# Seven block products for eight in a gated feed-forward layer, with its summed weights streamed from DRAM and GpSimd taken out of the work

## The chip, the cores and the metric

One core of one Trainium2 chip runs the kernel. The metric is device time in microseconds of one execution; the median of three runs stands for a kernel. A profiled execution of its own gives the trace.

## The reference, cut to what matters

Three stages follow each other on 2 x 3008 = 6016 tokens of 256 features, in float32.

```python
X = rfft(x, axis=1)                       # x: (2, 3008, 256)
Yr = Xr @ w_r - Xi @ w_i + b_r            # complex linear map in frequency space
Yi = Xr @ w_i + Xi @ w_r + b_i
y  = irfft(shrink(Yr, 0.01) + 1j * shrink(Yi, 0.01))
x  = y.reshape(6016, 256)
h  = x @ moe_w_in                         # first part, 2048 hidden
x  = (h * clip(h + 3, 0, 6) / 6) @ moe_w_out
g  = x @ moe2_w_gate                      # second part, 1536 hidden
out = (g / (1 + exp(-g)) * (x @ moe2_w_val)) @ moe2_w_out
```

`shrink(a, l)` is `sign(a) * max(abs(a) - l, 0)`.

## The kernel before, in words

The kernel has a Fourier stage (forward transform, complex linear map, inverse transform, up to about 172 us) and then two feed-forward parts. Tokens of the feed-forward parts come in 12 blocks: eleven of 512 and one of 384. Every product of the two parts is made of three float32r matmuls, from operands that are split in a high and a low half: low weight by high data, high weight by low data, high by high (`mm3`, lines 103 to 106). A weight tile is 128 x 128 and the moving operand is one block of up to 512 tokens.

The first part has 16 slices f of 128 hidden features. A unit (block, f) runs `project1` (line 386: two `mm3` into a PSUM tile `ph`, a Relu on ScalarE, a multiply on VectorE), then `lower` (line 434: the high half by a ScalarE copy, the low half by a subtraction), then `outp` (line 445: two `mm3` into the two accumulators `acc`). The second part has 12 slices, and `project2` (line 407) makes four `mm3` (gate and value, each over the two halves of the 256 input features), so with `outp` a unit takes 18 matmuls. In the loop at line 487 a unit's `outp` is issued after the `project` of the unit two later. `rounds` (line 459) lets the parts alternate: first part of block 0, first part of block 1, second part of block 0, first part of block 2, and so on. `post` (line 371) makes the input of a block of the first part from the Fourier stage's result, with 12 to 14 small float32 matmuls for each half of the features.

All weights come as 64-bit words and are converted on the chip (`Convert`, line 125): a load, a Square on ScalarE (the mask), four VectorE instructions of 256 columns (`words`, lines 152 to 156), a high half by a ScalarE copy, and a low half by a GpSimd subtraction (line 164). The 32 pieces of the first part's weights (`conv1`) are converted during the Fourier stage, one step in each `ln` (line 272) and in each late `pre`. The 36 pieces of the second part's weights (`conv2`) are converted one in each unit from the start of the first part, and while this lasts `lower` puts its subtraction on GpSimd (line 441). In the Fourier stage GpSimd also makes `yp`, the subtraction at the end of `ln` (line 293). All weights then stay in SBUF.

The order in which each engine works is the program order (the schedule is written out by hand). The Fourier stage goes through twelve steps p (`ORDER`, line 307): `ln(p, 0)`, `ia(p-1, 0)`, two halves of `s2(p+1)`, `ln(p, 1)`, `ia(p-1, 1)`. In `s2` (line 248) ScalarE makes the high half `xh` and its negative, VectorE the low half `xl`, and ScalarE the negative of `xl`; this last one is put ahead of the next function by `run` (line 265), so that the second half's `xh` stands behind it in ScalarE's queue.

Of the kernel before, what the change touches and what calls it, by code (L numbers as in the profile page):

```python
# [9 lines left out]
F32 = mybir.dt.float32  # L10
# [21 lines left out]
BLK = 512  # L32

# [41 lines left out]
def fourier_moe_kernel(ctx: ExitStack, tc: tile.TileContext, x, lin, bias, w1, w2, fwd1, inv2, fwd2,  # L75
# [6 lines left out]
    ps = ctx.enter_context(tc.tile_pool(name="ps", bufs=1, space=PSUM))  # L82
    dram = ctx.enter_context(tc.tile_pool(name="scratch", bufs=1, space=DRAM))
    Bd = [dram.tile([GW, NJ * DIM], F32, name=f"Bd{b}") for b in range(NB)]
    Cd = [dram.tile([GW, NJ * DIM], F32, name=f"Cd{b}") for b in range(NB)]

# [35 lines left out]
    w1p = pool(ctx, "w1", "right")  # L122
    W1, W2 = {}, {}

    class Convert:
# [21 lines left out]
        def words(self, i):  # L147
# [8 lines left out]
            v.scalar_tensor_tensor(out=tf, in0=m, scalar=LEAST * LEAST, in1=tf, op0=ALU.is_ge, op1=ALU.mult)  # L156
            self.full[i] = tf
# [114 lines left out]
    def ln(b, Q, h):  # L272
# [20 lines left out]
        nc.gpsimd.tensor_tensor(out=yp[b, Q, h], in0=yb, in1=yc, op=ALU.subtract)  # L293
# [51 lines left out]

    blocks = [(t, min(t + BLK, TOK)) for t in range(0, TOK, BLK)]

# [9 lines left out]
    ct, xs1, xs2, acc, state = {}, {}, {}, {}, {}  # L357
# [40 lines left out]
    def finish1(k, n):  # L398
        a = acc.pop((1, k))
        xs2[k] = pair(xb_p, "xb")  # L400
        for e in range(2):
            hi, lo = (t[:, e, :n] for t in xs2[k])
            nc.scalar.mul(hi, a[e][:, :n], 1.0 / 6.0)
            nc.vector.scalar_tensor_tensor(out=lo, in0=a[e][:, :n], scalar=1.0 / 6.0, in1=hi.bitcast(F32),  # L404
                                           op0=ALU.mult, op1=ALU.subtract)

    def project2(k, f, n):
        xh, xl = xs2[k]
        wh, wl = W2[f]
        pg = bank([128, BLK], "pg")  # L410
        pv = bank([128, BLK], "pv")
        for j, p in ((0, pg), (1, pv)):
            for dh in range(2):
                w = (slice(None), j, slice(dh * 128, dh * 128 + 128))
                mm3(p[:, :n], wh[w], wl[w], xh[:, dh, :n], xl[:, dh, :n], dh == 0, dh == 1)
        r = xs_p.tile([128, 512], F32, tag="r", name="r", bufs=3)
        nc.scalar.activation(r[:, :n], pg[:, :n], AF.Silu)  # L417
        nc.vector.tensor_tensor(out=r[:, :n], in0=r[:, :n], in1=pv[:, :n], op=ALU.mult)  # L418
        return r

    def finish2(k, n):
        a = acc.pop((2, k))
        t0 = k[0]
        for e in range(2):
            o = xs_p.tile([128, 512], F32, tag="r", name="osb", bufs=3)
            if e == 0:
                nc.scalar.copy(o[:, :n], a[e][:, :n])
            else:
                nc.vector.tensor_copy(o[:, :n], a[e][:, :n])
            nc.sync.dma_start(out[e * 128 : e * 128 + 128, t0 : t0 + n], o[:, :n])  # L430

    PART = {1: (KF1, project1, finish1, W1, 1), 2: (KF2, project2, finish2, W2, 2)}

    def lower(u):
        n = ntok(u[1])
# [4 lines left out]
        busy = conv1.done() and not conv2.done()  # L440
        (nc.gpsimd if busy else nc.vector).tensor_tensor(  # L441
            out=lo[:, :n], in0=g[:, :n], in1=hi[:, :n].bitcast(F32), op=ALU.subtract)
        state[u] = (hi, lo)

    def outp(u):
        part, k, f = u
        nf, _, finish, W, col = PART[part]
        n = ntok(k)
        if f == 0:
            acc[part, k] = [acc_bank([128, BLK], f"acc{e}") for e in range(2)]  # L450
# [4 lines left out]
        if f == nf - 1:  # L455
            finish(k, n)

    NBK = len(blocks)
    rounds = [(1, 0)]
    for n in range(NBK):  # L460
        if n + 1 < NBK:
# [84 lines left out]
```

## Time and profile before

| | |
|---|---|
| median of 3 runs | 1309.83 us (1308.58 to 1311.1) |
| the profiled execution | 1310.21 us, of which 1308.4 us are its span from first to last instruction |
| mean granted TensorE clock | 0.993 |
| busy: TensorE, VectorE, ScalarE, GpSimd | 98%, 51%, 42%, 11% of the span |

The profile's durations of matmuls overlap, because matmuls are pipelined, so a stretch in which TensorE is shown busy throughout can still hold more or fewer matmuls. The pace is read from the starts of successive matmuls.

### The profile page before, as it was taken

To read this page: it belongs to the slowest core of one execution; us is meant where nothing else is said; L and a number is where in the kernel's file an instruction comes from. 1 tells how busy PE (TensorE), PEld (TensorE's weight loads), DVE (VectorE), ACT (ScalarE), POOL (GpSimd) and SP (SyncE) were. 2 spreads that over 40 slices of the span, in tenths; PEclk is the share of its full clock that TensorE was granted. 3 is DMA by queue.
4 is the path that set the end of the run, shared out by engine and by line. 5 is a ranking of instruction groups with operands and counts; after the bars stand their busy time and mean duration, and the time that the engine had idled before them with its cause. 6 is when DMAs were issued, how large, how long until landed. Compare 5 with 4: busy or idle time off the path is not lost.

```text
span 1308.4 us, 15775 instructions
## 1 busy us (share of the span) xinstructions
PE 1280.3 (98%) x6124; PEld 1070.1 (82%) x6124; DVE 673.0 (51%) x1054; ACT 550.4 (42%) x982; POOL 149.9 (11%) x146
## 2 busy tenths in 40 slices
PE   7889999999999999999999999999999999999998
PEld 2689977678888888888888888888888888889888
DVE  2687889994543543534534434434434435435433
ACT  2345556563433433433433434434434424424332
POOL 1144457763000000000000000000000000000000
PEclk9899999999999999999999999999999999999999
DMA  8866532230100100001001001001001001000000
GB/s 281 272 210 201 171 116 79 79 91 1 35 1 1 38 1 16 20 1 38 1 1 35 1 1 38 1 1 35 1 1 35 1 1 32 1 1 17 1 17 13
DMA packets 33099, 61.42 MB, mean 47 GB/s; under 512 B 2928, under 2 KB 15568, under 8 KB 33024
## 3 DMA queue, kind: packets, MB, share of 16 engines
q1 hardware_dynamic: 26464, 53.43, 13.2%
q10 hardware_dynamic: 6336, 6.29, 1.4%
q8 instruction: 48, 0.79, 0.3%
q0 software_dynamic: 224, 0.69, 0.2%
q14 instruction: 27, 0.22, 0.1%
HBM read 41.66 MB, written 18.74 MB: 46 GB/s over the span
## 4 chain that ended last, share of the span: by engine, by line
PE 85%; DVE 9%; issue 3%; DMA 1%; ACT 1%; POOL 0%; SPq 0%; DVEq 0%; ACTq 0%; POOLq 0%
PE acc L105 10%; PE acc L106 10%; PE acc L104 10%; PE ph L106 5%; PE ph L104 5%; PE ph L105 5%; PE pg L104 5%; PE pg L106 5%; PE pv L104 5%; PE pg L105 5%; PE pv L106 5%; PE pv L105 5%; PE p L380 2%; DVE wt L153 2%; DVE wt L154 2%
## 5 line engine op out<-in xcount | busy, mean ns | idle before, releaser
L439 ACT CAST gh<-r 128x512 fp32r<-128x512 f32 (+1 forms) x336 | 205.5, 612 | 274.6 <-DVE r L418 156.6
L441 DVE TENSOR_TENSOR gl<-r,gh 128x512 fp32r<-128x512 f32 (+1 forms) x297 | 201.7, 679 | 174.5 <-ACT gh L439 173.6
L418 DVE TENSOR_TENSOR r<-r,pv 128x512 f32<-128x512 f32 (+1 forms) x144 | 97.4, 676 | 231.7 <-PE pv L106 231.7
L395 DVE SCALAR_TENSOR_TENSOR r<-r,ph 128x512 f32<-128x512 f32 (+1 forms) x192 | 129.7, 676 | 109.3 <-ACT r L394 109.3
L394 ACT ACTIVATE r<-ph,three 128x512 f32<-128x512 f32 (+1 forms) x192 | 130.3, 679 | 110.0 <-PE ph L106 101.8
L105 PE MATMUL acc<-gl,w1h 128*128 128x512 f32 (+1 forms) x384 | 149.9, 390 | 4.1 <-POOL gl L441 1.7
L104 PE MATMUL ph<-xah,w1l 128*128 128x512 f32 (+1 forms) x384 | 148.9, 388 | 0.0
L104 PE MATMUL acc<-gh,w1l 128*128 128x512 f32 (+1 forms) x384 | 147.8, 385 | 0.7 <-DVE xbl L404 0.7
L105 PE MATMUL ph<-xal,w1h 128*128 128x512 f32 (+1 forms) x384 | 148.2, 386 | 0.0
L106 PE MATMUL ph<-xah,w1h 128*128 128x512 f32 (+1 forms) x384 | 148.1, 386 | 0.0
L106 PE MATMUL acc<-gh,w1h 128*128 128x512 f32 (+1 forms) x384 | 147.9, 385 | 0.0
L417 ACT ACTIVATE r<-pg 128x512 f32<-128x512 f32 (+1 forms) x144 | 85.0, 590 | 147.1 <-PE pg L106 143.6
L104 PE MATMUL pg<-xbh,w2l 128*128 128x512 f32 (+1 forms) x288 | 112.6, 391 | 0.0
L106 PE MATMUL pg<-xbh,w2h 128*128 128x512 f32 (+1 forms) x288 | 110.9, 385 | 0.0
L104 PE MATMUL pv<-xbh,w2l 128*128 128x512 f32 (+1 forms) x288 | 110.8, 385 | 0.0
L105 PE MATMUL pg<-xbl,w2h 128*128 128x512 f32 (+1 forms) x288 | 110.8, 385 | 0.0
L106 PE MATMUL acc<-gh,w2h 128*128 128x512 f32 (+1 forms) x288 | 110.8, 385 | 0.0
L106 PE MATMUL pv<-xbh,w2h 128*128 128x512 f32 (+1 forms) x288 | 110.8, 385 | 0.0
L105 PE MATMUL acc<-gl,w2h 128*128 128x512 f32 (+1 forms) x288 | 110.8, 385 | 0.0
L105 PE MATMUL pv<-xbl,w2h 128*128 128x512 f32 (+1 forms) x288 | 110.7, 384 | 0.0
L104 PE MATMUL acc<-gh,w2l 128*128 128x512 f32 (+1 forms) x288 | 110.7, 384 | 0.0
L105 PEld LDWEIGHTS acc<-gl,w1h 128*128 128x128 f32 x384 | 72.0, 188 | 25.5 <-POOL gl L441 12.1
(66 smaller groups left out, 1903.4 us busy)
## 6 DMA issues: line engine op xcount, KB each, us to landing
st<-in_w SPq DMA_DIRECT2D x68, 256.0 KB, 2.7
x<-in_x SPq DMA_DIRECT2D x16, 384.0 KB, 5.5
Bd<-bs SPq DMA_DIRECT2D x16, 384.0 KB, 4.4
z<-Bd SPq DMA_DIRECT2D x12, 512.0 KB, 6.0
Cd<-cs ACTq DMA_DIRECT2D x12, 512.0 KB, 5.6
out_t<-osb SPq DMA_DIRECT2D x22, 256.0 KB, 2.0
ct<-Cd SPq DMA_DIRECT2D x6, 576.0 KB, 4.5
ct<-Cd SPq DMA_DIRECT2D x4, 672.0 KB, 4.8
```

Source lines behind the costliest of these rows:

```text
L104: nc.tensor.matmul(o, wl, xh, start=start, stop=False)
L105: nc.tensor.matmul(o, wh, xl, start=False, stop=False)
L106: nc.tensor.matmul(o, wh, xh, start=False, stop=stop)
L153: v.scalar_tensor_tensor(out=t, in0=L, scalar=29, in1=t, op0=ALU.logical_shift_right, op1=ALU.bitwise_or)
L154: v.scalar_tensor_tensor(out=t, in0=H, scalar=0xC0000000, in1=t, op0=ALU.bitwise_and, op1=ALU.bitwise_or)
L380: nc.tensor.matmul(p[:, a - k[0] : z - k[0]], ct[k][:, j - p0, eh * 128 : (eh + 1) * 128], inv2_sb[:, a - j * QN : z - j * QN], start=True ...
L394: nc.scalar.activation(r[:, :n], p[:, :n], AF.Relu, bias=three)
L395: nc.vector.scalar_tensor_tensor(out=r[:, :n], in0=r[:, :n], scalar=6.0, in1=p[:, :n], op0=ALU.min, op1=ALU.mult)
L417: nc.scalar.activation(r[:, :n], pg[:, :n], AF.Silu)
L418: nc.vector.tensor_tensor(out=r[:, :n], in0=r[:, :n], in1=pv[:, :n], op=ALU.mult)
L439: nc.scalar.copy(hi[:, :n], g[:, :n])
L441: (nc.gpsimd if busy else nc.vector).tensor_tensor(out=lo[:, :n], in0=g[:, :n], in1=hi[:, :n].bitcast(F32), op=ALU.subtract)
```

## The change

It does six things.

1. The first part runs over all blocks before the second part begins. Its result is stored as full float32 in a DRAM tensor `Xd` (two 256 KB stores for each block) and is loaded again, one pair of blocks at a time, for the second part. The last two blocks have 448 tokens each, in place of 512 and 384.
2. The second part takes pairs of blocks. For a slice f and a pair, gate and value by two halves of the input features form a 2 x 2 block matrix of weights, and two halves of the features by two blocks form a 2 x 2 block matrix of data. Their product is made of seven block products (Strassen, in Winograd's form) in place of eight, each an `mm3` as before, accumulated in three PSUM tags `P` (two banks), `Tb` and `Q`, with copies of intermediate sums in SBUF. `outp` is unchanged in kind: four `mm3` for a pair. So a `quad` (pair, f) takes 33 matmuls, where the two units took 36.
3. Sums of weights (four VectorE instructions of 128 columns for each slice) and their high and low halves are made once, during the first part, by one step in every second unit, and stored in DRAM tensors `Wd` (18 blocks of 128 x 128 for each slice, 1.18 MB). The second part loads a slice for each quad, 72 loads, into a ring of four buffers; the load for quad q+2 is issued at the start of quad q.
4. Sums of data (four VectorE subtractions, seven ScalarE copies and seven VectorE subtractions for each pair) are made during the pair before, at two places in each quad (`todo.send()`); those of the first pair are made in the last 28 units of the first part.
5. The subtractions on GpSimd go to VectorE: `Convert.low`, `yp`, and `lower` during the conversion.
6. PSUM and the first part's weights are released between the parts and taken again with new tags.

```diff
         def low(self, i):
-            nc.gpsimd.tensor_tensor(out=lo, in0=self.full.pop(i), in1=hi.bitcast(F32), op=ALU.subtract)
+            nc.vector.tensor_tensor(out=lo, in0=self.full.pop(i), in1=hi.bitcast(F32), op=ALU.subtract)
...
-        nc.gpsimd.tensor_tensor(out=yp[b, Q, h], in0=yb, in1=yc, op=ALU.subtract)
+        nc.vector.tensor_tensor(out=yp[b, Q, h], in0=yb, in1=yc, op=ALU.subtract)
...
+    pairs = [(t, min(t + 2 * BLK, TOK)) for t in range(0, TOK, 2 * BLK)]
+    blocks = [(a + (z - a) // 2 * i, a + (z - a) // 2 * (i + 1)) for a, z in pairs for i in range(2)]
...
-        busy = conv1.done() and not conv2.done()
-        (nc.gpsimd if busy else nc.vector).tensor_tensor(
-            out=lo[:, :n], in0=g[:, :n], in1=hi[:, :n].bitcast(F32), op=ALU.subtract)
+        low(lo[:, :n], g[:, :n], hi[:, :n])
...
+    units = [(k, f) for k in blocks for f in range(KF1)]
...
+            for f in range(KF2):                      # Convert2.steps, one step in every second unit
+                for what in range(3):
...
+                    self.words(i, self.full_of(i))
+                    yield
+                F = full.pop(f)
+                for o, x, y, op in ((4, 0, 3, ALU.add), (5, 4, 1, ALU.subtract), (6, 1, 0, ALU.subtract), (7, 2, 5, ALU.subtract)):
+                    nc.vector.tensor_tensor(out=F[:, o], in0=F[:, x], in1=F[:, y], op=op)
+                t = ring()
+                nc.scalar.copy(t[:, :7], F[:, 1:])
+                yield
+                O = full.pop((f, 2))
+                nc.scalar.copy(t[:, 14:16], O)
+                low(t[:, 7:14], F[:, 1:], t[:, :7])
+                yield
+                low(t[:, 16:], O, t[:, 14:16])
+                nc.sync.dma_start(Wd[f], t.bitcast(F32).rearrange("p a b -> p (a b)"))
+                yield
...
+    def fetch(q):
+        if q < len(quads):
+            slot[q] = ring()
+            nc.sync.dma_start(slot[q].bitcast(F32).rearrange("p a b -> p (a b)"), Wd[quads[q][1]])
...
+    w1_stack.close()
+    ps_stack.close()
...
+        def product(o, m, start=False):               # inside quad(q)
...
+            nc.tensor.matmul(o, wl, x[:, 0, :n], start=start, stop=False, skip_group_check=not start)
+            nc.tensor.matmul(o, wh, x[:, 1, :n], start=False, stop=False, skip_group_check=not start)
+            nc.tensor.matmul(o, wh, x[:, 0, :n], start=False, stop=True, skip_group_check=not start)
...
+        fetch(q + 2)
...
+        product(P, 1, start=True)
+        nc.scalar.copy(c1, P[:, :n])
+        product(T, 7, start=True)
+        nc.scalar.copy(c7, T[:, :n])
+        product(Q, 2, start=True)
+        nc.vector.tensor_tensor(out=v0, in0=Q[:, :n], in1=c1, op=ALU.add)
+        if before is not None:
+            (pb, fb), w, g = before
+            hi = split_hi(g[1], pb)
+            g[1] = (hi, split_lo(g[1], hi, pb))
+        product(P, 6)
+        nc.scalar.copy(cu, P[:, :n])
+        todo.send()
+        share(0, 0)
+        product(T, 4)
+        nc.vector.tensor_tensor(out=h, in0=T[:, :n], in1=cu, op=ALU.add)
+        nc.scalar.activation(s0[:, :n], h, AF.Silu)
+        share(0, 1)
+        product(P, 5)
+        nc.vector.tensor_tensor(out=h, in0=P[:, :n], in1=c7, op=ALU.add)
+        nc.scalar.activation(s1[:, :n], h, AF.Silu)
+        nc.vector.tensor_tensor(out=s0[:, :n], in0=s0[:, :n], in1=v0, op=ALU.mult)
+        hi = split_hi(s0, p)
+        g0 = (hi, split_lo(s0, hi, p))
+        todo.send()
+        share(1, 0)
+        share(1, 1)
+        product(P, 3)
+        nc.vector.tensor_tensor(out=s1[:, :n], in0=s1[:, :n], in1=P[:, :n], op=ALU.mult)
```

`share(t, e)` is one `mm3` of the quad before into accumulator (t, e); `split_hi` is a ScalarE copy and `split_lo` a VectorE subtraction.

## Rows read from the trace of the kernel before

**Rows 1.** The page: busy time and share of the span of each engine, number of instructions.

```profile
PE 1280.3 (98%) x6124; PEld 1070.1 (82%) x6124; DVE 673.0 (51%) x1054; ACT 550.4 (42%) x982; POOL 149.9 (11%) x146
```

**Rows 2.** Timeline of TensorE: start, duration, engine, line, operation; [idle before, releaser].

```profile
340.45 0.39 PE L104 MATMUL ph<-xah,w1l 128*128 128x512 f32 x1
...
343.17 0.39 PE L104 MATMUL ph<-xah,w1l 128*128 128x512 f32 x1
...
1284.14 0.33 PE L105 MATMUL pg<-xbl,w2h 128*128 128x384 f32 x1
...
1287.26 0.33 PE L105 MATMUL pg<-xbl,w2h 128*128 128x384 f32 x1
```

**Rows 3.** Timeline of TensorE, end of the Fourier stage to the second part's eighth slice.

```profile
171.44 1.40 PE L300 MATMUL p<-yp,n 128*128 128x256 f32 x4 [1.93 <-POOL yp L293]
172.28 0.99 PE L104 MATMUL ph<-xah,w1l 128*128 128x512 f32 x1
...
175.60 0.40 PE L105 MATMUL ph<-xal,w1h 128*128 128x512 f32 x1
...
304.62 1.65 PE L380 MATMUL p<-inv_sb,ct 96*128 96x10 f32 x14
```

**Rows 4.** Timeline, all engines, while the second part's weights are converted.

```profile
223.57 1.49 POOL L441 TENSOR_TENSOR gl<-r,gh 128x512 fp32r<-128x512 f32 x1 [0.79 <-POOL w2l L164]
223.94 1.40 DVE L156 SCALAR_TENSOR_TENSOR wt<-mask,wt 128x256 f32<-128x256 f32 x1
...
232.69 0.43 DVE L156 SCALAR_TENSOR_TENSOR wt<-mask,wt 128x256 f32<-128x256 f32 x1
...
236.02 0.50 PE L105 MATMUL acc<-gl,w1h 128*128 128x512 f32 x1 [0.98 <-POOL gl L441]
```

**Rows 5.** The chain that ended last, in the Fourier stage: start, duration, what.

```profile
95.93 0.87 PE p L300 x4
...
105.20 0.86 PE p L300 x4
...
150.90 0.61 DVE yb L289
...
160.37 0.61 DVE yb L289
```

**Rows 6.** Timeline of VectorE in one step of the Fourier stage.

```profile
126.76 0.68 DVE L289 TENSOR_TENSOR yb<-p,bias_sb 128x512 f32<-128x512 f32 x1
...
127.89 0.68 DVE L109 TENSOR_TENSOR xl<-p,xh 128x512 fp32r<-128x512 f32 x1
129.82 0.69 DVE L109 TENSOR_TENSOR xl<-p,xh 128x512 fp32r<-128x512 f32 x1 [1.25 <-ACT xh L259]
130.43 0.28 DVE L152 TENSOR_SCALAR wt<-st 128x256 uint32<-128x256 uint32 x1
...
132.01 0.68 DVE L289 TENSOR_TENSOR yb<-p,bias_sb 128x512 f32<-128x512 f32 x1
```

**Rows 7.** Groups by line and shape, whole span: count, busy us, mean ns, idle before.

```profile
L441 DVE TENSOR_TENSOR gl<-r,gh 128x512 fp32r<-128x512 f32 x269 | 186.1, 692 | 159.4 <-ACT gh L439 158.6
...
L418 DVE TENSOR_TENSOR r<-r,pv 128x512 f32<-128x512 f32 x132 | 90.8, 688 | 214.7 <-PE pv L106 214.7
...
L427 ACT COPY osb<-acc 128x512 f32<-128x512 f32 x11 | 6.5, 588 | 1.4 <-PE acc L106 1.2
```

**Rows 8.** Timeline of ScalarE: the Relu behind the matmuls of Rows 2.

```profile
342.07 0.69 ACT L394 ACTIVATE r<-ph,three 128x512 f32<-128x512 f32 x1 [0.66 <-PE ph L106]
```

**Rows 9.** DMA issues: count, KB each, median us from issue to landing.

```profile
ct<-Cd SPq DMA_DIRECT2D x4, 672.0 KB, 4.8
```

**Rows 10.** Stretches of 20 us: busy us (instructions) by engine, granted clock, DMA share, GB/s.

```profile
20.00:40.00 20.00, 12.70 (x39) 5.68 (x40) 5.95 (x11) 5.11 (x11) 0.00 (x0) 0.89 0.93 332
...
160.00:180.00 20.00, 18.07 (x102) 15.63 (x101) 17.40 (x29) 9.98 (x21) 9.38 (x10) 0.91 0.57 175
...
220.00:240.00 20.00, 17.71 (x72) 12.72 (x72) 19.42 (x32) 12.28 (x26) 13.86 (x12) 1.00 0.28 78
```

More of the change, by code (lines that the diff above doesn't have):

```diff
@@ L32 @@
 BLK = 512
+SLOT = 18
 EDGE = 480
@@ new lines, in fourier_moe_kernel, with operands, load, b @@
+    conv2 = Convert2([(w2[:, f, j], None, None) for f in range(KF2) for j in range(3)])
+    steps = conv2.steps()
+    B, raw = {}, {}
+    halves = [(z - a) // 2 for a, z in pairs]
+    xo = [cv, None]
+    def operands(p):
+        a, z = pairs[p]
+        n = halves[p]
+        def load():
+            raw[p] = cv.tile([128, 2, 2 * BLK], F32, tag="raw", name=f"raw{p}", bufs=1)
+            nc.sync.dma_start(raw[p][:, :, : z - a], Xd[:, :, a:z])
+        def b(k, t):
+            return raw[p][:, k, t * n : t * n + n]
+        B[p] = {}
+        T = {}
+        def sub(i, x, y):
+            T[i] = cv.tile([128, BLK], F32, tag="T", name=f"T{i}", bufs=3)
+            nc.vector.tensor_tensor(out=T[i][:, :n], in0=x(), in1=y(), op=ALU.subtract)
+        def hi(m, x):
+            B[p][m] = xo[p % 2].tile([128, 2, BLK], F32R, tag="xo", name=f"xo{m}", bufs=7)
+            nc.scalar.copy(B[p][m][:, 0, :n], x())
+        def lo(m, x):
+            low(B[p][m][:, 1, :n], x(), B[p][m][:, 0, :n])
+        def t(i):
+            return lambda: T[i][:, :n]
+        def r(k, j):
+            return lambda: b(k, j)
+        of = {1: r(0, 0), 5: t(1), 6: t(2), 4: t(4), 7: t(3), 2: r(1, 0), 3: r(1, 1)}
+        todo = [load, lambda: None]
+        subs = {5: (1, r(0, 1), r(0, 0)), 6: (2, r(1, 1), t(1)), 4: (4, r(1, 0), t(2)), 7: (3, r(1, 1), r(0, 1))}
+        for m, x in of.items():
+            if m in subs:
+                todo.append(lambda m=m: sub(*subs[m]))
+            todo.append(lambda m=m, x=x: hi(m, x))
+            todo.append(lambda m=m, x=x: lo(m, x))
+        return todo
@@ L487, in fourier_moe_kernel @@
+    def fetch(q):
+        if q < len(quads):
+            slot[q] = ring()
+            nc.sync.dma_start(slot[q].bitcast(F32).rearrange("p a b -> p (a b)"), Wd[quads[q][1]])
+    quads = [(p, f) for p in range(len(pairs)) for f in range(KF2)]
+    first = iter(operands(0))
     for n in range(len(units) + 2):
@@ L499, in fourier_moe_kernel, with sb @@
             conv1.step()
-        conv2.step()
+        elif n % 2 == 0:
+            next(steps, None)
+        left = len(units) + 2 - n
+        if left <= 28:
+            next(first, lambda: None)()
+        if left in (8, 4):
+            fetch(2 - left // 4)
+    assert next(steps, True) and next(first, None) is None
+    w1_stack.close()
+    ps_stack.close()
+    ps2 = ctx.enter_context(tc.tile_pool(name="ps2", bufs=1, space=PSUM))
+    p2 = pool(ctx, "p2", "right")
+    xo[1] = p2
+    def sb(tag, name, bufs):
+        return p2.tile([128, BLK], F32, tag=tag, name=name, bufs=bufs)
@@ L503, with __init__, send @@
+    class Todo:
+        def __init__(self):
+            self.steps = iter(())
+        def send(self):
+            next(self.steps, lambda: None)()
+    todo = Todo()
+    for q in range(len(quads) + 1):
+        if q < len(quads) and quads[q][1] == 0 and quads[q][0] + 1 < len(pairs):
+            todo.steps = iter(operands(quads[q][0] + 1))
+        quad(q)
 def kernel(x, w_r, w_i, b_r, b_i, moe_w_in, moe_w_out, moe2_w_gate, moe2_w_val, moe2_w_out):
```

171 lines of the change are left out of this document (109 added, 62 removed).

## The prediction

> **What bounds the kernel now.** I read the page first: TensorE is busy 98% of the span, no other engine over 51% [rows 1]. That share hides the pace, so the timeline of TensorE comes next, for starts of successive matmuls. In the undisturbed part 12 matmuls of 512 columns start in 343.17 - 340.45 = 2.72 us, 0.2267 us each, and 18 of 384 columns in 3.12 us, 0.1733 each [rows 2]. The difference is 0.417 ns a column, with 13 ns beside it for each matmul, so I reckon 0.200 us for 448 columns. At these paces the first part costs 192 x (11 x 0.2267 + 0.1733) = 512.0 us and the second 216 x (11 x 0.2267 + 0.1733) = 576.0 us. There TensorE alone sets the time.
>
> Two stretches are not of that kind. From the first `ph` matmul at 172.28 to the `post` at 304.62 there are two rounds of the first part and eight slices of the second, with their `outp` two units behind: 516 matmuls, 117.0 us, and two `post` halves of the length in [rows 3], 3.2 us after overlap. The stretch takes 132.3 us, so 12.1 are lost. Of these 1.7 are lost at the start: seven matmuls take 175.60 - 172.28 = 3.32 us instead of 1.59, right behind an idle time of 1.93 us [rows 3]. The other 10.4 are the conversion of the second part's weights: a VectorE instruction of 256 columns takes 0.43 us alone, but 1.40 us when it starts beside a GpSimd subtraction of 1.49 us, and ends just after it; TensorE then waits for the GpSimd low half [rows 4]. In such a stretch of 20 us 72 matmuls start, where the pace allows 88, though TensorE is shown busy 17.71 us [rows 10].
>
> The Fourier stage is the other. The chain of waits repeats there every 9.27 us through TensorE and later every 9.47 us through VectorE [rows 5]. So VectorE is about as near to the bound as TensorE.
>
> **The block products.** A quad takes 33 matmuls where two units took 36. Five pairs of 512-column halves and one of 448: 12 x 33 x (5 x 0.2267 + 0.200) = 528.0 us, against 576.0. Term: -48.0. The first part's matmuls cost 192 x (10 x 0.2267 + 2 x 0.200) = 512.0, as before, and the posts are the same work.
>
> This holds only if TensorE finds its operands in time, so I follow a quad in slots of one `mm3` (0.68 us): M1, M7, M2, M6, share, M4, share, M5, share, share, M3. A result can be read 0.26 us after the group's matmuls have issued (six from 340.45 end at 341.81, the Relu starts at 342.07) [rows 2, 8]. A ScalarE copy from PSUM takes 0.59, a VectorE addition from PSUM or a low half 0.69 [rows 7]. M6 adds into the bank that the copy `c1` reads: M1 ends at 0.68, the copy runs 0.94 to 1.53, M6 starts at 2.04; slack about 0.45. M5 needs `cu` (done 3.6) at 4.76. M3 needs the addition behind M5 (5.44): 5.70 to 6.39, and M3 starts at 6.80; slack about 0.35. The share of a quad's first half follows a quad later, with some 1.7 us to spare. In its queue VectorE has seven instructions of 0.69 and on average one more for `operands`, 5.5 of 7.48 us, and ScalarE seven of about 0.6. One send stands ahead of the addition behind M4 and the other ahead of the next quad's `v0`; neither reaches either slack. So I take no stall in the 72 quads; each 0.1 us of shortfall would cost 7.2 us.
>
> The first quad has no shares between its products: M5 waits about 0.2 for `cu` and M3 about 1.0 for its addition, +1.2. Before it the first part's last `outp` now waits for Relu, multiply, high and low half, where another block's matmuls covered them: +0.3. After the last quad two shares (1.2 us) cover only part of multiply, high half and low half (about 2.8 us behind M3): +1.4. A last store of 448 columns in place of 384: +0.2. New banks and buffers between the parts are last used by work that TensorE has passed; nothing, at most 2.
>
> **The weight stream.** 72 loads of 1.18 MB, one for each 7.48 us, are 158 GB/s. A load is issued two quads, 14.9 us, ahead, on SP's queue, where it can stand behind four stores of a finished pair, whose last copy comes some 2 us into the next quad, and beside one 1 MB load of `Xd` for each pair. The slowest price is a lone load of 672 KB in 4.8 us with its latency [rows 9], which scales to 8.4 us; the fastest is a stretch at 332 GB/s [rows 10], 3.6 us. I take the second as nearer, as several loads are in flight in both: hidden. The `Xd` stores and the output stores are work for an SP queue with nothing urgent in it.
>
> **Conversion in the first part.** In two units VectorE has four instructions of 0.69 and at most one step; a `words` step takes 132.01 - 130.43 = 1.58 us when GpSimd is still [rows 6]. That is 4.35 of 5.44 us (24 matmuls), and a step's delay fits the two units between a unit's `project` and its `outp`. The step with four sums (about 1.3 us) puts a copy of 896 columns into ScalarE's queue and leaves some 0.6 us. Of the 10.4 us I take 9.8 back; bounds 6.0 and 10.4. The slow start stays.
>
> **GpSimd's work on VectorE in the Fourier stage.** One step p from VectorE's queue, undisturbed: `yb` and `yc` 1.13 (126.76 to 127.89), first `xl` to second 1.93, of which 1.25 waits for ScalarE, second `xl` 0.61, `words` 1.58 [rows 6]. The wait stays however late VectorE is: the second half's `xh` stands in ScalarE's queue behind the negative of the first half's `xl`. To each `ln` the change adds `yp`, 0.69 less 0.08 of overlap plus some 0.1 behind `yc`, and one low half of 256 columns, between 0.35 (half of 0.69) and 0.43 [rows 4, 7], say 0.37. So a step takes 2 x (1.58 + 1.13 + 0.71 + 0.37) + 1.93 + 0.61 = 10.1 us, with GpSimd's disturbance already gone. Ten of the twelve steps are of this kind, five from 9.27 and five from 9.47: 5 x 0.85 + 5 x 0.65 (10.12 unrounded), +7.5. In the first two the gain and the addition come out even. Bounds: -1.0, if the wait takes up the additions and the later five fall to 9.27; +11, if the first two grow as well.
>
> **Sum.** -48.0 - 9.8 + 7.5 + 0.3 + 1.2 + 1.4 + 0.2 = -47.2. The profiled execution took 1310.2 us in all, 1308.4 of them its span, so 1263.0; it stands 0.4 above the median of the runs, so 1263 for the median, rounded.
>
> **Rivals.** (1) The round trips in a quad don't fit. For: slacks of 0.35 and 0.45 us are one late instruction. Against: the durations are from the same kinds of instruction. A shortfall of 0.3 us costs 72 x 0.3 = 21.6: 1285; the gain is gone at 0.65.
>
> (2) The other side: the weights don't come in time. If loads behaved like the lone one in [rows 9], 8.4 us each and one after the other, a quad would take 8.4 us and the kernel 1263 + 72 x 0.92 = 1329, slower. It decides from 47 / 72 = 0.65 us a quad, that is 8.13 us or 145 GB/s. Against it stands the stretch at 332 GB/s.
>
> (3) TensorE's clock falls in the second part. Behind an idle time of 1.93 us it stood at 0.91 in its stretch, part of it at 1.2 GHz [rows 3, 10]; with idle times of 0.98 us [rows 4] it stayed at 1.00 (2.4 GHz) throughout [rows 10]. At the low level seven matmuls took 3.32 us [rows 3], so a quad of 33 takes about 8.2 us longer, at most; six such quads undo the gain. Half of all quads at the low level give about 1560. A quad by my slots has no idle time at all, so the traces speak against it. The Trainium skill (TensorE: Matmul & The Clock Gate, section "A second HAM failure mode: psum-queue depth-cycling") says that a kernel of 512-column matmuls which cycles through PSUM banks in each iteration can make TensorE idle so often that its clock goes up and down. By that rule this rival would be the likely one; the kernel before cycles five banks and shows 1.00, so the trace does not bear it out.
>
> **Numbers.** Forecast 0.78, rival 1 0.13, rival 2 0.06, rival 3 0.03. The forecast's own bounds run from 1252 (-48.0 - 10.4 - 1.0 + 1.5) to 1272 (-48.0 - 6.0 + 11 + 5); the range adds the nearer half of rival 1 and drops the edges: 1253 to 1282. A difference of 0.2%, 2.6 us, is about what a measurement here can tell from none. Faster by more: the forecast, most of rival 1 (0.115) and a part of rival 2 (0.01), 0.90; the same: 0.02; slower: the rest, 0.08.
>
> **What would show it.** Of the changed kernel: starts 0.2267 us apart through whole quads, 7.48 us from M1 to M1; no idle time at M6 or M3 (rival 1 would show VectorE or ScalarE releasing them), none at M1 behind a load (rival 2), clock 1.00 (rival 3); VectorE instructions of 256 columns at 0.43 everywhere; steps of about 10.1 us in the Fourier stage, with the first `ph` matmul near 180; the first part about 546 us long (512.0, eleven pairs of posts at 2.6 to 3.2, the slow start and the bits left over). The prediction is wrong most likely if a wait that I set at nothing occurs once in each quad, or if the Fourier stage finds room that I deny it.

## The result, and the profile after

The changed kernel takes 1262.1 us in the median (1261.14 to 1262.98, 4 runs), the kernel before 1310.46 beside it: a ratio of 0.9632, 95% interval 0.9616 to 0.9649. The forecast was 1263. The profiled execution took 1262.49 us, 1260.7 of them its span, at a mean granted clock of 0.992.

The page's line of busy times, to be read beside [rows 1]:

```profile
PE 1233.4 (98%) x5908; PEld 1037.2 (82%) x5908; DVE 847.2 (67%) x1491; ACT 681.2 (54%) x1216; POOL 6.3 (0%) x15
```

TensorE's share is the same 98%, of a shorter span, with 216 matmuls less (3 in each of 72 quads). The timeline of TensorE in a steady quad, from M1 to the next M1, with M3 between them:

```profile
797.95 0.39 PE L614 MATMUL P<-xo,slot 128*128 128x512 f32 x1
...
804.75 0.39 PE L614 MATMUL P<-xo,slot 128*128 128x512 f32 x1
...
805.43 0.39 PE L614 MATMUL P<-xo,slot 128*128 128x512 f32 x1
```

That is 805.43 - 797.95 = 7.48 us for 33 matmuls, 0.2267 each, and no row has an idle time. All that TensorE waited for after the Fourier stage is in its list of waits (us in total, times, longest; the rows of the Fourier stage and the small waits for `gl` are left out):

```profile
PE acc L110 <- ACT gh L425: 1.0, 1, 1.0
PE P L614 <- DVE g L684: 0.8, 1, 0.8
PE P L614 <- ACT x L415: 0.8, 1, 0.8
...
PE acc L110 <- ACT gh L638: 0.5, 1, 0.5
```

Each comes once: at the start of the first part, in the first quad, at the change of parts, after the last quad. No wait recurs with the quads and none is behind a weight load, whose issues and median landing time are:

```profile
slot<-Wd SPq DMA_DIRECT2D x72, 1152.0 KB, 5.0
```

Two stretches of 20 us, one from the conversion in the first part (as the last line of [rows 10]) and one from the second part; columns as there:

```profile
220.00:240.00 20.00, 20.00 (x90) 16.57 (x89) 14.06 (x26) 11.37 (x19) 0.00 (x0) 1.00 0.48 160
760.00:780.00 20.00, 20.00 (x90) 16.57 (x89) 14.25 (x24) 12.14 (x22) 0.00 (x0) 1.00 0.50 177
```

Where 72 matmuls started in 20 us there are now 90 instructions of TensorE, and the clock is 1.00, its 2.4 GHz level, in both.

The Fourier stage, which [rows 5, 6] showed before: the chain that ended last, and VectorE's timeline in one step.

```profile
77.13 0.86 PE p L310 x4
...
86.38 0.87 PE p L310 x4
...
95.75 0.86 PE p L310 x4
...
165.85 0.87 PE p L310 x4
```

```profile
102.52 0.69 DVE L115 TENSOR_TENSOR xl<-p,xh 128x512 fp32r<-128x512 f32 x1 [1.24 <-ACT xh L269]
```

Two steps are 9.25 and 9.37 us long, then come seven of (165.85 - 95.75) / 7 = 10.01. VectorE's instructions of 256 columns take 0.43 or less everywhere, and the wait of 1.25 us for `xh` is still there. The end of the stage and the first matmuls of the first part in TensorE's timeline, beside [rows 3]:

```profile
174.70 1.10 PE L310 MATMUL p<-yp,n 128*128 128x256 f32 x4 [0.69 <-DVE yp L303]
175.45 0.58 PE L110 MATMUL ph<-xah,w1l 128*128 128x512 f32 x1
...
180.96 0.49 PE L110 MATMUL acc<-gh,w1l 128*128 128x512 f32 x1 [1.05 <-ACT gh L425]
```

The first `ph` matmul starts at 175.45, 3.2 us later than before and not 7.5. VectorE's own queue shows the step better than the chain does. The first half's `xl` of the first and of the last of ten steps, before and after:

```profile
71.07 0.68 DVE L109 TENSOR_TENSOR xl<-p,xh 128x512 fp32r<-128x512 f32 x1
...
156.17 0.68 DVE L109 TENSOR_TENSOR xl<-p,xh 128x512 fp32r<-128x512 f32 x1
```

```profile
70.54 0.68 DVE L115 TENSOR_TENSOR xl<-p,xh 128x512 fp32r<-128x512 f32 x1
...
160.68 0.68 DVE L115 TENSOR_TENSOR xl<-p,xh 128x512 fp32r<-128x512 f32 x1
```

Nine steps take 85.10 us before and 90.14 after, 9.46 and 10.02 each, and in both kernels all nine are alike to 0.15 us.

### The profile page after: what moved, and what is told of

It is laid out like the page before. It is cut to its first block, busy times and chain, and to the rows that moved or that the text cites. A ratio compares the mean times of both kernels' runs of the same rounds, so it can differ in the third digit from the quotient of the medians.

```text
span 1260.7 us, 15970 instructions
## 1 busy us (share of the span) xinstructions
PE 1233.4 (98%) x5908; PEld 1037.2 (82%) x5908; DVE 847.2 (67%) x1491; ACT 681.2 (54%) x1216; POOL 6.3 (0%) x15
## 4 chain that ended last, share of the span: by engine, by line
PE 91%; DVE 4%; ACT 2%; DMA 2%; issue 1%; SPq 0%; DVEq 0%; ACTq 0%
PE acc L111 12%; PE acc L112 12%; PE acc L110 12%; PE ph L110 7%; PE ph L112 7%; PE ph L111 7%; PE P L614 5%; PE P L616 5%; PE P L615 5%; PE Tb L614 3%; PE Tb L616 3%; PE Tb L615 3%; PE p L392 2%; PE Q L614 1%; PE Q L616 1%; PE Q L615 1%
## 5 line engine op out<-in xcount | busy, mean ns | idle before, releaser
L115 DVE TENSOR_TENSOR gl<-r,gh 128x512 fp32r<-128x512 f32 (+1 forms) x192 | 130.2, 678 | 75.0 <-ACT gh L425 73.2
L425 ACT CAST gh<-r 128x512 fp32r<-128x512 f32 (+1 forms) x192 | 117.5, 612 | 98.3 <-DVE r L407 98.3
L115 DVE TENSOR_TENSOR gl<-s,gh 128x512 fp32r<-128x512 f32 (+1 forms) x144 | 97.3, 676 | 49.0 <-ACT gh L638 48.8
L614 PE MATMUL P<-xo,slot 128*128 128x512 f32 (+1 forms) x288 | 111.2, 386 | 1.5 <-DVE g L684 0.8
L111 PE MATMUL acc<-gl,slot 128*128 128x512 f32 (+1 forms) x288 | 111.1, 386 | 0.5 <-DVE gl L115 0.5
L110 PE MATMUL acc<-gh,slot 128*128 128x512 f32 (+1 forms) x288 | 111.1, 386 | 0.5 <-ACT gh L638 0.5
L616 PE MATMUL P<-xo,slot 128*128 128x512 f32 (+1 forms) x288 | 110.9, 385 | 0.0
L615 PE MATMUL P<-xo,slot 128*128 128x512 f32 (+1 forms) x288 | 110.9, 385 | 0.0
L112 PE MATMUL acc<-gh,slot 128*128 128x512 f32 (+1 forms) x288 | 110.9, 385 | 0.0
L680 ACT ACTIVATE s<-g 128x512 f32<-128x512 f32 (+1 forms) x72 | 44.9, 623 | 93.8 <-DVE g L678 93.8
L638 ACT CAST gh<-s 128x512 fp32r<-128x512 f32 (+1 forms) x144 | 88.2, 612 | 1.0 <-DVE s L694 0.8
L110 PEld LDWEIGHTS acc<-gh,w1l 128*128 128x128 f32 x384 | 72.1, 188 | 15.0 <-ACT gh L425 1.5
L112 PEld LDWEIGHTS ph<-xah,w1h 128*128 128x128 f32 x384 | 72.1, 188 | 13.8
```

The lines of the kernel that those rows point to most:

```text
L110: nc.tensor.matmul(o, wl, xh, start=start, stop=False)
L111: nc.tensor.matmul(o, wh, xl, start=False, stop=False)
L112: nc.tensor.matmul(o, wh, xh, start=False, stop=stop)
L115: nc.vector.tensor_tensor(out=o, in0=full, in1=hi.bitcast(F32), op=ALU.subtract)
L425: nc.scalar.copy(hi[:, :n], g[:, :n])
L614: nc.tensor.matmul(o, wl, x[:, 0, :n], start=start, stop=False, skip_group_check=not start)
```

## The experiments

The kernel before took 1310.76, 1309.97 and 1310.11 us beside the three groups of runs, so times stand side by side to within 1 us. Intervals of ratios are 95%. In some kernels line numbers are one to four higher than in the changed kernel.

### The eighth product put back

```diff
         product(P, 3)
+        product(P, 3)
```

The seventh product of each quad is issued twice, so that the value half of the output gets it twice: an mm3 more with no result waited for that was not waited for before.

> The changed kernel with its last block product, product(P, 3), issued twice in each quad: an eighth product, so the sums in the output are not the reference's. Theory (TensorE alone sets the pace of the second part, 0.2267 us for each 512-column matmul): 3 more matmuls in 72 quads cost 60 x 0.68 + 12 x 0.61 = 48 us, so about 1310 us. Rival (a quad also waits for VectorE and ScalarE, so that a part of the eighth product hides): under 1295 us.

Measured: 1309.14 us, ratio 0.9988 (0.9979 to 0.9997), 47.0 us above the changed kernel. In its trace a steady quad takes 8.16 us in place of 7.48, the price of three matmuls. So three matmuls in each quad are worth what TensorE's pace makes them worth, to within 1 us of 48. The other parts of the change together come out about even.

### A late addition in each quad

```diff
         nc.vector.tensor_tensor(out=h, in0=T[:, :n], in1=cu, op=ALU.add)
         s0 = sb("s", "s0", 3)
...
         product(P, 5)
+        nc.vector.tensor_tensor(out=s0[:, :n], in0=s0[:, :n], in1=v0, op=ALU.mult)
         h = sb("h", "g1", 3)[:, :n]
         nc.vector.tensor_tensor(out=h, in0=P[:, :n], in1=c7, op=ALU.add)
...
-        nc.vector.tensor_tensor(out=s0[:, :n], in0=s0[:, :n], in1=v0, op=ALU.mult)
```

> In the quads of the second part, the multiply of silu(v0) with v0 is put ahead of the addition behind M5 on VectorE. In a steady quad of the changed kernel the silu ends at 803.66, the multiply would then end at about 804.3 and the addition at about 805.0, where M3 is due at 804.75, so that M3 comes about 0.3 us late with its semaphore. Theory (the round trips of the quad are followed rightly, and an addition that comes late is paid for in each quad): some 0.2 to 0.4 us in each of 72 quads, 14 to 29 us, so 1276 to 1291 us, with M3 waiting for VectorE in each quad. Rival (TensorE has enough else in its queue or VectorE orders itself so that nothing is late): 1261 to 1264 us. If the theory holds, the forecast's first rival had the right price and failed only by its slack.

Measured: 1295.79 us (1293.96 to 1298.01), ratio 0.989 (0.9874 to 0.9906): 33.7 us more, 0.47 for each quad in the mean. The timelines of VectorE and TensorE in one quad of this kernel:

```profile
804.78 0.68 DVE L685 TENSOR_TENSOR g<-P,c 128x512 f32<-128x512 f32 x1
```

```profile
805.01 0.39 PE L112 MATMUL acc<-gh,slot 128*128 128x512 f32 x1
805.52 0.50 PE L614 MATMUL P<-xo,slot 128*128 128x512 f32 x1
805.86 0.40 PE L615 MATMUL P<-xo,slot 128*128 128x512 f32 x1
806.10 0.40 PE L616 MATMUL P<-xo,slot 128*128 128x512 f32 x1
```

The addition ends at 805.46 and M3 starts at 805.52, where the pace would have it at 805.24: 0.28 us late, as expected. But the next two matmuls start 0.34 and 0.24 apart in place of 0.2267, and the next few a little above it, so that nearly every quad grows by 0.42 to 0.46 and not by 0.3 (the first two grow by 3.5 together, behind a wait of 2.3 us). The first rival had its mechanism right and its price too low: in this loop a wait of 0.28 us cost some 0.15 us more than its idle time. In the changed kernel the same place has about 0.4 us to spare (its addition runs from 803.59 to 804.28, M3 starts at 804.75), which is why nothing is seen there.

### The weight stream: doubled, doubled from another queue, and later

```diff
             nc.sync.dma_start(slot[q].bitcast(F32).rearrange("p a b -> p (a b)"), Wd[quads[q][1]])
+            nc.sync.dma_start(slot[q].bitcast(F32).rearrange("p a b -> p (a b)"), Wd[quads[q][1]])
```

> Each weight sum of the second part is loaded twice into its slot, one transfer behind the other, so that the second part draws twice the bytes (about 316 GB/s) and a load takes about 10 us in place of 5.0. Theory (the stream is hidden behind 14.9 us of lead, two quads): 1261 to 1264 us, no wait of TensorE behind a load. Rival (the stream is near its limit, or the transfers take bandwidth or SBUF access from what else runs): each quad waits for its slot, over 1275 us.

Measured: 1357.21 us (1355.83 to 1359.98), ratio 1.0361 (1.0344 to 1.0377). The theory fell: 95 us more. In TensorE's list of waits, and at one change of pair in the timelines of SyncE's queue and of TensorE:

```profile
PE P L615 <- ACT cu L674: 47.0, 5, 10.2
PE P L615 <- DMA slot<-Wd: 20.7, 17, 2.5
```

```profile
1035.15 0.39 SPq L563 DMA_DIRECT2D slot<-Wd  x1
1042.59 0.32 SPq L564 DMA_DIRECT2D slot<-Wd  x1
...
1043.62 9.94 SPq L634 DMA_DIRECT2D out_t<-osb  x4
...
1054.98 0.80 PE L615 MATMUL P<-xo,slot 128*128 128x512 f32 x1 [10.04 <-ACT cu L674]
1055.57 0.63 PE L616 MATMUL P<-xo,slot 128*128 128x512 f32 x1
1056.00 0.63 PE L617 MATMUL P<-xo,slot 128*128 128x512 f32 x1
```

A second load into the same slot can only be issued when the first has landed, so SyncE stands 7.4 us between the two issues (1035.15 to 1042.59), and a quad needs 7.5. The stores of the finished pair stand behind that in the same queue, so VectorE's copy of the next output waits for a buffer that a store still reads; the multiply of `s` stands behind that copy, ScalarE's high half waits for the multiply, and `cu` stands behind the high half. Five changes of pair cost 47.0 us, and behind the one shown TensorE works at its 1.2 GHz level for a while (starts 0.43 us apart from 1055.57 to 1060.26). To part the queue's order from the bytes, the second load was issued from GpSimd's empty queue:

```diff
             nc.sync.dma_start(slot[q].bitcast(F32).rearrange("p a b -> p (a b)"), Wd[quads[q][1]])
+            nc.gpsimd.dma_start(slot[q].bitcast(F32).rearrange("p a b -> p (a b)"), Wd[quads[q][1]])
```

> Each weight sum of the second part is again loaded twice into its slot, but the second load is issued from GpSimd's queue, which is empty, and not from SyncE's. With both loads on SyncE's queue the time was 1357 us: SyncE stood 7.4 to 9.0 us behind each first load, the next load and the stores of a pair stood behind it, and at each change of pair TensorE stood about 10 us and went on at half its clock. Theory (the queue's order does it, the bytes do not): the same 316 GB/s without SyncE standing, two loads of about 5 to 8 us in 14.9 us of lead, so 1262 to 1270 us and no wait of 10 us at a change of pair. Rival (the bytes do it, transfers and stores get too slow): still over 1300 us.

Measured: 1313.34 us (1302.67 to 1319.07, 10 runs), ratio 1.0009 (0.9984 to 1.0034). Neither theory holds alone: 44 of the 95 us were the order in SyncE's queue, 51 are still there. In this kernel's list of waits, and in a stretch of 130 us (columns as in [rows 10]):

```profile
PE P L615 <- DMA slot<-Wd: 35.6, 23, 7.0
```

```profile
730.00:860.00 130.00, 120.18 (x511) 97.17 (x512) 81.44 (x127) 70.29 (x122) 8.46 (x16) 0.96 0.83 312
```

The waits of 10 us behind `cu` are gone (2.1 us in all, the longest 1.1), and TensorE waits for the loads themselves, 23 times, up to 7.0 us, while the DMA engines move 312 GB/s at a busy share of 0.83. A load's median landing time is 7.2 us, against 5.0. Since a slot's second load is issued only when its first has landed, two in a row take 14.4 of the 14.9 us of lead; whether the remaining 51 us are the price of the bytes or of that order within a slot was not tried. The Trainium skill (DMA: Bandwidth & Descriptors, section "Issuing engines are not separate DMA queues") says that transfers of all engines run on the same 16 DMA engines, so that issuing from several saves only the issuing sequencer's time, usually a small one. The loads' longer landing time agrees; the 44 us don't agree with "small", because here a sequencer stood behind a wait with other transfers behind it.

The third run left the bytes alone and took one quad of the lead away:

```diff
-        fetch(q + 2)
+        fetch(q + 1)
...
-        if left in (8, 4):
-            fetch(2 - left // 4)
+        if left == 8:
+            fetch(0)
```

> Each weight sum is issued one quad ahead (7.48 us) in place of two (14.9 us); all else is as in the changed kernel. Theory (a load lands 5.0 us after its issue in the median, and is late only where it stands behind stores or the next inputs at a change of pair, five times, where it lands up to 8.4 us after its issue): 1262 to 1268 us. Rival (a lead of one quad does not hide the stream, as the forecast's second rival has it): each quad waits, over 1275 us.

Measured: 1264.86 us (1264.2 to 1266.52), ratio 0.966 (0.9644 to 0.9675), as the theory has it, 2.8 us above the changed kernel. TensorE's list of waits shows where:

```profile
PE P L614 <- DMA slot<-Wd: 1.4, 5, 0.4
```

Five waits: one in the kernel's second quad, four in the third quad of a pair, whose load is due at the start of the second quad and stands behind the stores of the pair before. So the second quad of lead buys about 3 us, and the rest of the stream is hidden by one.

### GpSimd's two jobs, apart

Its work in the Fourier stage given back to it (`Convert.low` and `yp`):

```diff
-            nc.vector.tensor_tensor(out=lo, in0=self.full.pop(i), in1=hi.bitcast(F32), op=ALU.subtract)
+            nc.gpsimd.tensor_tensor(out=lo, in0=self.full.pop(i), in1=hi.bitcast(F32), op=ALU.subtract)
...
-        nc.vector.tensor_tensor(out=yp[b, Q, h], in0=yb, in1=yc, op=ALU.subtract)
+        nc.gpsimd.tensor_tensor(out=yp[b, Q, h], in0=yb, in1=yc, op=ALU.subtract)
```

> The changed kernel with two subtractions given back to GpSimd, yp and the low half of the first part's weights; nothing else. Theory (VectorE's queue sets the Fourier stage's later steps, at 10.02 us each against 9.27 to 9.47 before): the first ph matmul comes at 172 to 173 us again instead of 175.45, and the time falls by about 3 us to 1259. Rival (what GpSimd takes away comes back as blocked VectorE instructions and as a longer idle time of TensorE at the stage's end): 1261 to 1263 us, no gain.

Measured: 1259.88 us (1258.32 to 1260.6), ratio 0.9608 (0.9593 to 0.9623). The first `ph` starts at 173.16 against 175.45: 2.3 us earlier, and the whole is 2.2 faster.

One half of its work in the first part given back, the product's low half (the weights' low half stays on VectorE), with the conversion still in every second unit:

```diff
+    on_pool = [False]
...
-        low(lo[:, :n], g[:, :n], hi[:, :n])
+        (nc.gpsimd if on_pool[0] else nc.vector).tensor_tensor(
+            out=lo[:, :n], in0=g[:, :n], in1=hi[:, :n].bitcast(F32), op=ALU.subtract)
...
+        on_pool[0] = conv1.done() and n < 152
```

> The changed kernel with the low half of the first part's product made on GpSimd in the units in which the second part's weights are converted, as the kernel before had it; the steps still come in every second unit. Theory A (the 10.4 us that were lost before come from GpSimd's subtraction blocking VectorE): the units with a step lose some 0.4 us each, 36 steps with four word instructions, about 15 us, so 1272 to 1280 us. Theory B (they come from a step in each unit, too dense for VectorE): under 3 us lost, 1262 to 1265 us.

Measured: 1266.38 us (1264.77 to 1267.14), ratio 0.9658 (0.9639 to 0.9676): 4.3 more, between the two theories. In the timelines of the engines:

```profile
231.07 1.40 DVE L167 SCALAR_TENSOR_TENSOR full<-mask,wt 128x256 f32<-128x256 f32 x1
...
283.19 0.94 ACT L503 CAST slot<-full 128x896 fp32r<-128x896 f32 x1 [1.74 <-DVE full L501]
...
286.12 0.50 PE L111 MATMUL acc<-gl,w1h 128*128 128x512 f32 x1 [0.64 <-POOL gl L428]
```

VectorE's last instruction of a `words` step takes 1.40 us again in most of the 36 steps, but no unit with such a step loses time: TensorE's pace holds behind 231.07. The time is lost at three places (286.12, 426.50 and 567.47), each in a step with the four sums, where ScalarE's copy of 896 columns stands ahead of the high half and GpSimd's low half then takes 1.28 us in place of VectorE's 0.69. So theory A had its price from a mechanism that costs nothing here.

And the other half of what the kernel before did there, a step of the conversion in each unit, with the subtractions on VectorE:

```diff
-        elif n % 2 == 0:
+        else:
             next(steps, None)
```

> The changed kernel with a conversion step of the second part's weights in each unit of the first part instead of each second one; GpSimd stays out. Theory A (GpSimd's blocking was the loss): VectorE needs 7.1 us for six steps and 8.3 us for six units, 15.4 of 16.3 us, so at most 2 us are lost, 1262 to 1264 us. Theory B (density was the loss): about 10 us, 1270 us or more.

Measured: 1266.91 us (1266.35 to 1267.83), ratio 0.9664 (0.9649 to 0.9678): 4.8 more, again between. Here too it loses the time in the step with the four sums: at seven places behind the start of the first part (near 203, 257, 290, 310, 327, 345 and 399 us) matmuls of `acc` come 0.3 to 0.9 us late, each behind ScalarE's copy of 896 columns. In the kernel before, which has no such step, the loss looks otherwise. The first two matmuls of an `acc` group in TensorE's timeline, in the stretch of [rows 4]:

```profile
224.58 0.39 PE L104 MATMUL acc<-gh,w1l 128*128 128x512 f32 x1
225.11 0.50 PE L105 MATMUL acc<-gl,w1h 128*128 128x512 f32 x1
```

They start 0.53 us apart and the third follows at 225.45, 0.4 us lost, and so it goes in nearly every unit from 208 to 271 us. Neither run brings that back. GpSimd's low half together with a step in each unit, as the kernel before has them, was not run.

### The wait in the Fourier stage

ScalarE's negative of the first half's `xl` is queued behind the second half's copies, so that the second half's `xl` on VectorE need not wait for it:

```diff
-        later.append(lambda: nc.scalar.mul(nlo, X[b, Q][1][:, dh, :, 2 * K2 :].bitcast(F32), -1.0))
+        held.append(lambda: nc.scalar.mul(nlo, X[b, Q][1][:, dh, :, 2 * K2 :].bitcast(F32), -1.0))
+        if dh == 1:
+            later.extend(held)
+            held.clear()
...
-    later = []
+    later, held = [], []
```

> In the Fourier stage, ScalarE's negative of the first half's xl is queued behind the second half's copies, so that the second half's xl on VectorE no longer waits 1.24 us for xh in each step. Theory (that wait is what makes the seven steps 10.02 us long where TensorE's own work is 9.25 to 9.37): the steps fall to about 9.3, some 4 to 5 us in all, so 1257 to 1259 us and the first part begins near 171. Rival (VectorE's own work sets the pace, and the wait only moves): no step shortens, 1261 to 1264 us. If the negative itself becomes late for the matmuls that read it, TensorE waits for ScalarE: over 1264 us.

Measured: 1252.12 us (1251.62 to 1252.21), ratio 0.9555 (0.9541 to 0.9569): 10.0 less than the changed kernel, twice what was expected. VectorE's timeline in one step, and the chain that ended last:

```profile
104.91 0.69 DVE L115 TENSOR_TENSOR xl<-p,xh 128x512 fp32r<-128x512 f32 x1 [0.20 <-ACT xh L269]
```

```profile
97.58 0.87 PE p L313 x4
...
153.18 0.87 PE p L313 x4
```

The wait of 1.24 us is 0.20 now, and all steps are (153.18 - 97.58) / 6 = 9.27 us long. The first `ph` starts at 165.58, 9.9 us earlier. Of these 5.2 are the seven steps (7 x 0.75); 0.9 are the end of the stage, where `yp` no longer comes late; the other 3.7 were gained earlier: the `z` matmuls that stand at 77.83 in the changed kernel stand at 74.15 here, for 2.2 of which a wait of 2.58 us for `xl` in an early step answers, which shrank to 1.23, and one of 0.87, which went away. Another 1.6 are the 18 matmuls behind these waits: in the changed kernel they start 0.21 us apart (granted clock 0.53 from 74 to 77, a mean over its two levels), here 0.12 apart at 1.00. The expectation had counted only the seven steps.

The same with GpSimd's work in the Fourier stage given back to it (both edits as above):

> The negative of the first half's xl is held back as in the run before with 1252.1 us, and in the Fourier stage yp and the words' low parts go back to GpSimd. GpSimd there was worth 2.2 us where the negative was not held back. Theory (with the negative held back TensorE sets the Fourier steps at 9.27 us and no engine's load matters any more): 1251 to 1253.5 us. Rival (VectorE's load is a cost of its own): about 1250 us.

Measured: 1256.11 us (1255.58 to 1256.69), ratio 0.9591 (0.9576 to 0.9606): 4.0 more than without GpSimd, which neither side had. In the timelines of GpSimd, VectorE and TensorE in an early step, and in a stretch at the start of the first part:

```profile
64.60 2.54 POOL L174 TENSOR_TENSOR w1l<-wt,w1h 128x256 fp32r<-128x256 f32 x3
...
65.70 0.84 DVE L161 SCALAR_TENSOR_TENSOR wt<-st,wt 128x256 uint32<-128x256 uint32 x1
...
70.33 0.39 PE L110 MATMUL p<-linh,xl 128*128 128x256 f32 x1 [2.24 <-DVE xl L115]
...
76.16 2.02 PE L264 MATMUL p<-m,z 128*128 128x128 f32 x16 [1.75 <-DMA z<-Bd]
```

```profile
175.00:180.00 5.00, 5.00 (x16) 3.90 (x16) 2.59 (x4) 2.29 (x4) 0.11 (x1) 0.68 0.00 0
```

The repeated steps are 9.27 us long here too, as the theory has it; the loss lies outside them. The first `ph` comes at 167.60, 2.0 later than without GpSimd, and all of that is there at the `z` matmuls of 76.16, which stand at 74.15 without GpSimd: TensorE waits 2.24 us for `xl` in place of 1.23, behind word instructions of VectorE that take 0.84 beside GpSimd's subtractions in place of 0.42, and then 1.75 for a load of `z` in place of 0.66. In the first part's first 12 us another 2.4 are lost: a wait of 1.42 for `gh` in place of 0.65, and behind it a stretch with 16 matmuls in 5 us at a granted clock of 0.68, a mean over its two levels. So GpSimd's help is worth 2.2 us where VectorE sets the repeated steps; where TensorE sets them it is worth nothing there, and its disturbance at the two ends of the stage costs 4.0.

### The blocks of 448 columns

```diff
-    blocks = [(a + (z - a) // 2 * i, a + (z - a) // 2 * (i + 1)) for a, z in pairs for i in range(2)]
+    blocks = [(t, min(t + BLK, TOK)) for t in range(0, TOK, BLK)]
```

> The first part goes back to eleven blocks of 512 tokens and one of 384, as the kernel before has it; the second part keeps its pairs. Theory (a 448-column matmul costs 0.2067 us in the first part where 512 and 384 columns cost 0.2267 and 0.1733 us): the last 896 tokens cost 0.4000 us for each pair of matmuls in place of 0.4134, over 192 such pairs 2.6 us less, so 1259 to 1260 us. Rival (the pitch of 0.2067 is a wait at the end of the first part and not the price of the size): 1261.5 to 1264 us.

Measured: 1260.33 us (1259.77 to 1262.62), ratio 0.9625 (0.9608 to 0.9641); by the runs alone it can't be told from the changed kernel. By the traces the first part, from the first `ph` to the first quad, takes 721.68 - 174.70 = 546.98 us in place of 724.37 - 175.45 = 548.92: 1.9 of the 2.6 expected (the rest is lost again at its change of parts).

The last run has this edit together with the negative held back:

> The negative held back (it gave 10 us) together with the first part's blocks of 512 and 384 tokens (they gave 1.8 us), which touch different stages. Theory: both add up, 1250 to 1250.8 us. Rival (the start of the first part or the change to the second part takes the second gain back): 1252 us.

Measured: 1250.36 us (1247.93 to 1253.26), ratio 0.9548 (0.9527 to 0.9568): the lowest median, some 12 us below the changed kernel, though its runs overlap with those of the kernel with the negative held back alone (1251.62 to 1252.21). Its first part takes 546.63 us, against 548.50 in the kernel with the negative held back alone, 1.9 less again.

## Why the prediction was right

| term | predicted | measured |
|---|---|---|
| block products, 33 matmuls for 36 | -48.0 | -48.0 by the pace in the trace, -47.0 by the eighth product put back |
| 448 columns at 0.200 us | 0 | +2.6 and +1.1 |
| conversion in the first part, with its start | -9.8 | -10.6 (12.6 lost before, 2.0 now) |
| Fourier stage | +7.5 | +3.2 |
| change of parts | +0.3 | +1.2 |
| first quad | +1.2 | +1.5 |
| after the last quad | +1.4 | +2.1 |

**The quad.** After the first quad no round trip is late in any quad; those of 512 columns take 7.48 us each, as forecast. The slack at M3 that the slots gave as 0.35 us is 0.4 in the trace, and the late addition shows that it is real: an addition that came 0.28 us late there cost 33.7 us.

**The weight stream.** It is hidden, with room: one quad of lead less costs 2.8 us. The second rival's condition, a quad's load every 8.1 us or more, was about met when each slot was loaded twice (the second loads of 1001 to 1043 us are issued 7.8 to 9.4 us apart), and the kernel was then slower than before, as that rival had it; what the rival did not see is that most of the waiting (47.0 us against 20.7) would come through the stores queued behind.

**The clock.** It is 1.00 through the second part. The third rival's ground, the cycling through PSUM banks, gave no fall here, though a quad goes through `P`, `Tb`, `Q` and the accumulators in turn and to `P` four times. The falls that these runs show stand behind waits: the 10.04 us one above is followed by matmuls 0.43 us apart.

**Conversion.** In the stretch of [rows 10] nothing is lost any more. The prediction put the loss down to GpSimd blocking VectorE, and so to TensorE's wait for the low half. The size was right; the mechanism is not shown. With GpSimd's low half given back, VectorE is blocked as before and TensorE does not wait for it, and both that run (4.3 us) and a step in each unit (4.8) lose their time in the step with the four sums, which the kernel before does not have. What made nearly every unit lose 0.4 us before, GpSimd's work, the denser steps or the two together, stays open. The size of the loss was read a little low: the two `post` halves of that stretch, at 193.20 and 200.02, put 1.35 us each between matmuls and not 1.6, so 12.6 were lost and not 12.1. The "slow start" of 1.7 us is gone as such (the granted clock is 1.00 there), but the first `acc` group waits for its high and low half: 20 intervals from 175.45 to 182.02 take 6.57 us in place of 4.53, so 2.0 us are lost at the same place in another way.

**The Fourier stage** is the step that failed in size: "Ten of the twelve steps are of this kind, five from 9.27 and five from 9.47". A step's new length was right (10.12 forecast, 10.02 measured, with the 1.24 us wait in it), but the old one was not: 9.27 is what the chain shows while TensorE, which entered behind, runs at its own pace, and VectorE's queue had 9.46 from the first of these steps. So the change adds 0.56 to each of nine steps, 5.0 us, and VectorE enters them 0.5 earlier, which leaves +4.5. TensorE shows it late: it runs two more steps of 9.25 and 9.37 until it has caught up, and then seven of 10.01 in which it waits for `xl`. The same +4.5 stands at the time at which TensorE is free for the last `yp` product (171.44 - 1.93 in [rows 3], 174.70 - 0.69 above); then `yp` on VectorE is late by 0.69 and not by 1.93 as on GpSimd, -1.3. Both terms of the long step are shown: without the wait behind the negative the steps fall to TensorE's 9.27 with VectorE's work unchanged, and without the added work, in the run with GpSimd given back, VectorE's step is 9.46 again with the wait unchanged.

**448 columns.** The interpolation to 0.200 us was wrong on the dear side. TensorE's timeline in the first and in the second part:

```profile
718.23 0.37 PE L110 MATMUL ph<-xah,w1l 128*128 128x448 f32 x1
...
720.71 0.37 PE L110 MATMUL acc<-gh,w1l 128*128 128x448 f32 x1
...
1241.60 0.36 PE L110 MATMUL acc<-gh,slot 128*128 128x448 f32 x1
...
1244.64 0.36 PE L110 MATMUL acc<-gh,slot 128*128 128x448 f32 x1
```

12 matmuls take 2.48 us, 0.2067 each, and 15 take 3.04, 0.2027 each. Over 384 matmuls of the first part that is 384 x 0.0067 = 2.6 us, over 396 of the second 1.1.

**The edges.** TensorE's timeline at the change of parts and the end:

```profile
721.95 0.37 PE L110 MATMUL acc<-gh,w1l 128*128 128x448 f32 x1
...
724.37 0.47 PE L614 MATMUL P<-xo,slot 128*128 128x512 f32 x1 [0.76 <-ACT x L415]
...
1252.34 0.36 PE L616 MATMUL P<-xo,slot 128*128 128x448 f32 x1
...
1256.83 0.36 PE L112 MATMUL acc<-gh,slot 128*128 128x448 f32 x1
```

Six intervals to the first quad take 2.42 us in place of 1.24: the first `P` lies in a bank from which ScalarE still copies the first part's result, the "new banks" that the prediction set at nothing, at most 2. The first quad, 21 matmuls to 730.61, takes 6.24 in place of 4.76; the last 12 matmuls 4.49 in place of 2.43. All three are of the size foreseen and somewhat above it.

The terms as measured, -48.0 + 3.7 + 3.2 + 1.2 + 1.5 + 2.1, come to -36.3; the two profiled executions differ by 1262.49 - 1310.21 = -47.7. That leaves -11.4, of which 10.6 are the conversion's and 0.8 are assigned to no row. So the total agrees to 0.5 us in part by luck: a Fourier stage 4.3 us better than forecast stood against 5.6 us of pitch and edges.

## What to carry to other kernels

Where one engine runs at its pace without idle time, work taken from it was worth its pace to within 1 us of 48 here, provided every round trip has some tenths of a microsecond to spare; count that slack per iteration, because 0.28 us of lateness cost some 0.44 in nearly each of 72. When two engines take turns at being the slowest, read each engine's own step from its own queue: the chain of waits shows the one that is behind. Before giving an engine's work to another, look for a wait in the second engine's queue that is only a matter of order: moving one ScalarE instruction of each step gave 10 us, more than any choice between GpSimd and VectorE. A stream's margin is set by what stands behind it in its queue as much as by its bytes, so test it by doubling it and from a second queue.

## What the runs showed of the hardware that was not expected

- A 448-column matmul costs 0.2067 us in the first part and 0.2027 in the second, where 512 columns cost 0.2267 and 384 cost 0.1733 [rows 2]. The price is not linear in the columns, and it differs between two places with the same shapes; why was not tried.
- Behind an idle time of 0.28 us the next matmuls start 0.34 and 0.24 us apart before the pace of 0.2267 returns, with the granted clock at 1.00.
- Twice the weight stream ran at 312 GB/s with the DMA engines 0.83 busy and a load landing in 7.2 us in the median, against 177 GB/s, 0.50 and 5.0 us.
- Whether the clock is granted at the start of the first part differs from kernel to kernel: a stretch at 0.68 with GpSimd and the negative held back, 1.00 with GpSimd alone, where TensorE had idled 1.95 us just before. What tells these apart stays open.
